# A fused linear-attention and FFN block: another order of transposes, late FFN units and query products

## The chip, the cores and the metric

One core of a Trainium2 chip runs the whole kernel. Its engines work side by side and meet through semaphores: TensorE (matrix products and transposes; PE in the profile, its weight loads PEld), VectorE (DVE), ScalarE (ACT), GpSimd (POOL) and SyncE (SP, which issues the DMA transfers). The metric is the device time of one execution in microseconds. Before the change it is 151.27 us, the median of three runs (151.26 to 151.32).

## What is computed

A token matrix x (2048 tokens, width 448) is layer-normalised, and three things are summed: x itself, a linear attention with 16 heads of width 28, and an FFN of width 1792.

```python
xn = _layernorm(x, axis=-1)
return x + _A_ref(xn, A_wqkv, A_w_phi, A_wo) + _B_ref(xn, B_w1, B_w2)
# A, for each head: pq = q @ w_phi, pk = k @ w_phi
phi_q = concat([softmax(pq), softmax(-pq)]);  phi_k = concat([softmax(pk), softmax(-pk)])
kv  = einsum("bhsf,bhsd->bhfd", phi_k, v);    z = einsum("bhsf->bhf", phi_k)
num = einsum("bhqf,bhfd->bhqd", phi_q, kv);   den = einsum("bhqf,bhf->bhq", phi_q, z) + 1e-6
A   = (num / den) @ wo
# B: silu(xn @ w1) @ w2
```

The key-value sums run over all tokens, so no attention output can be formed until the last keys are in.

## The kernel before

**Tiles.** The 2048 tokens are 16 tiles of 128, taken as 8 pairs. TensorE works with its rows in two halves, upper and lower 64, each with its own weights, so one "step" is two products that run side by side into two neighbouring PSUM banks. A contraction over 448 columns takes seven steps in two passes, 4 and then 3 (`contract`, L476); the second pass waits until the first is through. PSUM has eight banks of 512 fp32 columns, and nearly all waits of TensorE are for a bank that ScalarE or VectorE hasn't emptied yet.

**Stages on TensorE, in order.** First, each pair is normalised on VectorE (`ln_stats`, `ln_norm`, L617 to L634; for pairs 0 and 1 `lnz_norm`, L651), transposed on TensorE (`xnT_tr`) and evicted to the buffer xnT (`ln_ev`, `lnz_ev`), while FFN1 units (`ffn1_single`, `ffn1_chunk`) use the pairs that are ready; each unit is emptied by a SiLU on ScalarE. In the same stretch the weights w_phi are folded into those of queries and keys (`fold_tr`, `fold`). Second, for each pair the key, value and query projections (`k_macro`, `q_group`, `q_half`), exponentials on ScalarE, key softmax on VectorE and GpSimd, and key-value sums in one PSUM bank (`k_acc`). Third, the middle: the last FFN1 units ("late units"), the key-value sums transposed (`kv_transpose`) and evicted to KVZ, and the query products of pairs 0 and 1 (`q_products`). Fourth, for each pair the FFN's second product and the output projection, accumulated in one bank pair and stored (`out_pair`, `out_last`), with the query products two pairs ahead.

**Query products and their division.** `q_products(p)` writes, for tile t of the pair, 8 steps into the banks 2 + 2t and 3 + 2t. `q_divide(p)` then works on VectorE: reciprocal (L1145), Dd, den, rden, Gq (to L1155), and one large product from PSUM into the SBUF buffer o_both (L1160). For pair 0 it does all of this for one tile after the other, for pair 1 the factors for both tiles and then the large product by tile, for later pairs everything for both tiles. The large product empties the banks. GpSimd then sums the two softmax halves (L1182).

**What sets the order.** A small planner (`schedule`, L218) places every operation with rough costs; each engine runs its list in that order and waits for semaphores where a dependency crosses engines. On TensorE the planner has little to choose, as written-out lists (`order0`, L871 to L880; `mid`, L931; `chain`, L1056 to L1066 and L1265) fix the sequence through order-only dependencies. On VectorE and ScalarE it chooses, except where such a dependency (`odeps`) ties two operations. The late units are `u[0]` to `u[7]`; `u[i][0]` holds the first pass of unit i (for `u[3]` and later 4 steps of 512 columns), `u[i][1]` the second pass (3 steps). `uu[0]` to `uu[3]` are the query products of pair 0 tile 0, pair 0 tile 1, pair 1 tile 0, pair 1 tile 1.

**Other lines that matter.** `tr1` (L869) are the eight transposes of pair 1, four for each tile; `tr2` and `tr3` (L878) the seven of pairs 2 and 3. Transposes of one pair need different column pieces of the normalised tiles, which VectorE writes one by one. `ln_later` (L884) adds the later pairs; pairs 4 and 5 use the same banks for their transposes. Transfers `q_move` (L1024) rearrange query rows inside SBUF; `moved` (L1267) hangs their waits on late units. SyncE ends with one wait for each output slot (L1340).

```python
order0 += [a[0], b[0], a[1], b[1][:2], c[0], b[1][2:], tr1[:4], c[1][:-1], d[0], tr1[4:], c[1][-1:], d[1]]   # L871
order0[-2:] = [tr2, c1[:4], tr3, c1[4:], d1]                                                                 # L880
chain += [u[0][0], u[1][0], u[0][1], u[2][0], u[1][1], u[2][1], kv, u[3][0], kv_tr, u[3][1], u[4][0], uu[0], # L1265
          u[4][1], u[5][0], uu[1], u[5][1], u[6][0], uu[2], u[6][1], u[7][0], uu[3], u[7][1]]
```

Of the kernel before, what the change touches and what calls it, by code (L numbers as in the profile page):

```python
# [332 lines left out]
def bass_parallel_sum__linear_kernel_hedgehog__dense_activation_silu__prompt_kernel(  # L333
# [10 lines left out]
    S, D, H, DH, FF = 2048, 448, 16, 28, 1792  # L344
# [11 lines left out]
    with es:  # L356
# [303 lines left out]
        def lnz_bank(p, t, j):  # L660
            return 6 if p else ((4, 0) if t == 0 else (6, 2))[j // 2]

# [66 lines left out]
        def ln_pair(p, one_by_one=False, ev=True):  # L729
            t0, t1 = 2 * p, 2 * p + 1  # L730
            for t in (t0, t1):
                ln_stats(t)
                if one_by_one:
                    ln_rstd(t, t + 1)
            if not one_by_one:
                ln_rstd(t0, t1 + 1)
            ln_norm(p, t0)
            ln_norm(p, t1)
            b0 = {2: 0, 3: 2, 6: 0, 7: 0}.get(p, 6)
            ln_tr(p, [0, 1, 2, 3, 4, 5, 6], b0, 448 if p == 7 else 0)  # L740
            if ev:
                ln_ev(p, 0, 7, b0, "act" if p in LN_ACT else "dve")
# [69 lines left out]
        def fold_tr(w0):  # L812
            for w in range(w0, w0 + 3):
                for kt in range(4):
                    c = ((w - w0) * 4 + kt) * 64
                    c0 = 0 if w == 0 else 112 * w - 64
                    trs([(bank16[6 + h][:, c:c + 64], wraw[r, kt, c0:c0 + 128], r)
                         for h, r in ((0, UP), (1, LO))], "wT_tr")
            for h in range(2):
                src = bank16[6 + h][:, 0:768].rearrange("p (w k u) -> p w k u", w=3, k=4)  # L820
                dst = wT[:, w0:w0 + 3, :].rearrange("p w (k b u) -> p w b k u", b=2, u=64)[:, :, h]
                copy_dve(dst, src, "wT_ev", d_dve(768, 2))

        def fold(kt):
            bA, bB = banks[6], banks[7]
# [21 lines left out]
        banks_ = iter((4, 0, 2, 4, 0, 2, 4, 6))  # L847
        evp, passes, ln_late = [], [], []
# [44 lines left out]
        def last_xn(ops):  # L893
            return [o for o in ops if o.name == "xn"][-1].id
# [10 lines left out]
        ffn1_chunk(2, 2, 0, 4, (2, 4, 0))  # L905
        tr5, later5 = ln_later(5, early_dve)
        ftr = []
        for i in range(3):
            ffn1_chunk(2, 2, 4 + 2 * i, 6 + 2 * i, (2, 4, 0))
            ftr.append(marked(fold_tr, 3 * i))  # L910
        unit_no[0] = 0
        ffn1_chunk(2, 4, 10, FT, (0, 2, 4, 2))
        ffn1_chunk(4, 2, 0, 2, (4,))
        tr6, later6 = ln_later(6, last_xn(later4), False)
# [11 lines left out]
        for kt in range(4):  # L926
            if kt:
                ffn1_chunk(4, 4, 1 + kt, 2 + kt, (0, 2, 4))
            folds.append(marked(fold, kt))
# [18 lines left out]
        def k_macro(p):  # L948
            sl = p % NEK
            kbk = {1: 4, 2: 6, 7: 6}.get(p, 2)  # L950
            k12 = proj(p, lambda r, k: wqk_sb[r, k, 1, :, 0:56], kbk, "pk_mm")
# [24 lines left out]
        def k_acc(p):  # L976

            sl, ops = p % NEK, []
            for t in range(2):
                first, last = p == 0 and t == 0, p == NPAIR - 1 and t == 1  # L980
                E3 = Ek[sl][:, t, :].rearrange("p (s c) -> p s c", s=2)
                for c in range(4):
                    parts = []
                    for i in range(4):
                        h = 4 * c + i
                        parts.append((banks[4][VW * i:VW * i + VW, 56 * c:56 * c + 56].rearrange("p (s f) -> p s f", s=2),
                                      vaug[sl][:, t, h, :], E3[:, :, h * DH:h * DH + DH], first and c == 0, last))
                    ops.append(mms(parts, "kv_mm", 50.0, 32))
            return ops

        def q_group(ch, c):
            qb = {1: 2, 2: 4, 6: 2}.get(4 * ch + c, 6)
            done = contract([(lambda r, b: xnT[r, b, 4 * ch:4 * ch + 4, :].rearrange("p a c -> p (a c)"),
# [7 lines left out]
        def q_half():  # L1001


            qb, done = 6, []
            for q in range(2):
# [71 lines left out]
        def kv_transpose():  # L1077

            kvT = scr[:, 64:64 + 4 * 112]
            bA = banks[4][:, 0:4 * 56].rearrange("p (a f) -> p a f", a=8)[:, :, None, :].broadcast_to([128, 8, 2, DH])  # L1080
            dA = kvT.rearrange("p (a i f) -> p a i f", a=8, i=2)
# [4 lines left out]
            for s in range(2):  # L1086
                for c in range(4):
                    parts = []
                    for j in range(2):
                        r, o = slice(64 * j, 64 * j + 64), 64 + 112 * c + 56 * s - 64 * j  # L1090
                        parts.append((bank16[4 + j][:, (4 * s + c) * 64:(4 * s + c + 1) * 64], scr[r, o:o + 128],
                                      ident[r, 64 * j:64 * j + 64]))
# [8 lines left out]
            for j, eng in ((0, "dve"), (1, "act")):  # L1101
                r = slice(64 * j, 64 * j + 56)
                src = bank16[4 + j][r, 0:512].rearrange("p (a h d) -> p a h d", a=8, h=2)[:, :, :, 0:DV]
# [211 lines left out]
        def emit_engine(ename, eng):  # L1315
# [24 lines left out]
            if ename == "sp":  # L1340
                for i in range(len(out_sems)):
                    if out_cnt[i] > 0:
                        eng.wait_ge(out_sems[i], 16 * out_cnt[i])

# [48 lines left out]
```

## Time and profile before

| what | value |
|---|---|
| median of three runs | 151.27 us |
| the profiled execution | 151.52 us |
| its span, first to last instruction | 149.7 us |
| TensorE busy | 146.1 us |
| VectorE busy | 100.2 us |
| ScalarE busy | 72.5 us |
| GpSimd busy | 56.4 us |
| mean granted TensorE clock | 0.999 |

The profile is one execution, recorded by the hardware. Times in it count from the first instruction. A row of the timeline reads: start, length, engine, source line, operation, output<-inputs, shapes, number of instructions merged into the row, and in brackets the idle time of that engine before it with what ended it. A matrix product's end is modelled, and consecutive products overlap in the pipeline, so TensorE's progress is read from starts: the next group's start less this group's start. A row of the chain reads: start, length, engine, output, line. L448 is the helper that issues all products in halves, L461 the one for transposes, L467 every ScalarE operation, L471 every VectorE copy.

### The profile page before, as it was taken

To read this page: it belongs to the slowest core of one execution; us is meant where nothing else is said; L and a number is where in the kernel's file an instruction comes from. 1 tells how busy PE (TensorE), PEld (TensorE's weight loads), DVE (VectorE), ACT (ScalarE), POOL (GpSimd) and SP (SyncE) were. 2 spreads that over 40 slices of the span, in tenths; PEclk is the share of its full clock that TensorE was granted. 3 is DMA by queue.
4 is the path that set the end of the run, shared out by engine and by line. 5 is a ranking of instruction groups with operands and counts; after the bars stand their busy time and mean duration, and the time that the engine had idled before them with its cause. 6 is when DMAs were issued, how large, how long until landed. Compare 5 with 4: busy or idle time off the path is not lost.

```text
span 149.7 us, 5611 instructions
## 1 busy us (share of the span) xinstructions
PE 146.1 (98%) x2530; PEld 91.6 (61%) x2530; DVE 100.2 (67%) x192; ACT 72.5 (48%) x83; POOL 56.4 (38%) x86
## 2 busy tenths in 40 slices
PE   7999999999999999999999999999999999999992
PEld 6888889557764444444486545555555555555672
DVE  1888898885428899777992677839393939392203
ACT  3647756657799887779488654202020202022000
POOL 7133130210102779876991064270707060614000
PEclk9999999999999999999999999999999999999999
DMA  4999373100004332342201000010101010101012
GB/s 118 352 245 262 90 243 87 49 4 0 4 0 127 123 125 66 89 125 40 44 8 16 4 0 4 0 66 0 66 0 66 0 68 0 66 0 66 0 61 66
DMA packets 9426, 10.29 MB, mean 69 GB/s; under 512 B 1626, under 2 KB 9018, under 8 KB 9402
## 3 DMA queue, kind: packets, MB, share of 16 engines
q1 hardware_dynamic: 9098, 9.71, 22.6%
q8 instruction: 20, 0.33, 0.9%
q10 hardware_dynamic: 304, 0.21, 0.5%
q14 instruction: 4, 0.03, 0.1%
HBM read 7.37 MB, written 1.84 MB: 61 GB/s over the span
## 4 chain that ended last, share of the span: by engine, by line
PE 94%; DVE 3%; issue 0%; DVEq 0%
PE psum L448 91%; PE psum L461 3%; DVE wraw L1160 1%; DVE R L1145 0%; DVE rden L1152 0%; DVE out_raw L1211 0%; DVE Gq L1153 0%; DVE Dd L1147 0%; DVE den L1149 0%; PE psum L1096 0%; DVEq L1333 0%
## 5 line engine op out<-in xcount | busy, mean ns | idle before, releaser
L448 PE MATMUL psum<-w_sb,hT 64*128 64x448 bf16 (+2 forms) x504 | 46.5, 328 | 0.0
L448 PE MATMUL psum<-xnT,w_sb 64*128 64x256 bf16 (+2 forms) x600 | 46.3, 297 | 0.0
L467 ACT ACTIVATE hT<-psum 128x1024 bf16<-128x1024 f32 (+1 forms) x29 | 28.2, 994 | 14.1 <-PE psum L448 11.8
L1182 POOL TENSOR_TENSOR xn_sb<-wraw 128x448 bf16<-128x448 f32 (+4 forms) x39 | 20.7, 562 | 36.3 <-DVE wraw L1160 28.3
L448 PEld LDWEIGHTS psum<-xnT,w_sb 64*128 64x128 bf16 x600 | 27.9, 94 | 8.6
L448 PEld LDWEIGHTS psum<-w_sb,hT 64*128 64x128 bf16 x504 | 22.5, 94 | 16.8
L467 ACT ACTIVATE oT<-psum 128x896 bf16<-128x896 bf16 x8 | 7.3, 917 | 40.2 <-PE psum L461 40.2
L971 POOL TENSOR_TENSOR scr<-scr,Rk 128x1792 bf16<-128x1792 bf16 (+2 forms) x8 | 19.2, 2409 | 11.4 <-DVE Rk L965 7.9
L1160 DVE TENSOR_TENSOR wraw<-psum,Gq 128x1792 f32<-128x1792 f32 (+1 forms) x10 | 16.4, 1650 | 0.8
L467 ACT ACTIVATE EqT<-psum 128x1024 bf16<-128x1024 f32 x14 | 13.6, 1022 | 4.0 <-PE psum L448 4.0
L1211 DVE TENSOR_TENSOR out_raw<-psum,x_sb 128x896 bf16<-128x896 f32 (+2 forms) x9 | 8.8, 980 | 9.5 <-PE psum L448 9.4
L1145 DVE RECIPROCAL R<-psum 128x64 f32<-128x64 f32 (+1 forms) x9 | 4.6, 512 | 15.3 <-PE psum L448 15.3
L448 PE MATMUL psum<-wv_sb,xnT 64*128 64x448 bf16 x112 | 13.9, 349 | 0.0
L448 PE MATMUL psum<-wo_sb,oT 64*128 64x448 bf16 (+2 forms) x126 | 13.6, 328 | 0.0
L448 PE MATMUL psum<-wqk_sb,xnT 64*128 64x448 bf16 x112 | 13.4, 349 | 0.0
L625 POOL TENSOR_TENSOR rstd<-ve,neghalf 128x2 f32<-128x2 f32 (+1 forms) x9 | 6.0, 661 | 19.1 <-DVE ve L624 19.1
L448 PE MATMUL psum<-xnT,wqk_sb 64*128 64x512 bf16 (+1 forms) x112 | 13.0, 378 | 0.0
L963 DVE TENSOR_REDUCE Sk<-scr 128x64 f32<-128x1792 bf16 (+1 forms) x8 | 12.3, 1534 | 0.2
L610 DVE BATCH_NORM_STATS2 st<-x_sb 128x6 f32<-128x448 bf16 x16 | 9.8, 617 | 3.4 <-DMA x_sb<-in_A_x_dram 3.4
L467 ACT ACTIVATE scr<-psum 128x896 bf16<-128x896 f32 x12 | 10.3, 912 | 2.2 <-PE psum L448 1.8
L471 DVE CAST scr<-psum 128x896 bf16<-128x896 f32 x6 | 6.5, 1081 | 5.8 <-PE psum L448 5.8
L448 PEld LDWEIGHTS psum<-wo_sb,oT 64*128 64x128 bf16 x126 | 5.9, 94 | 4.8 <-ACT oT L467 0.2
(78 smaller groups left out, 136.5 us busy)
## 6 DMA issues: line engine op xcount, KB each, us to landing
out_dram<-out_raw SPq DMA_DIRECT2D x7, 224.0 KB, 1.9
w_sb<-in_B_w_dram SPq DMA_DIRECT2D x3, 448.0 KB, 3.3
x_sb<-in_A_x_dram SPq DMA_DIRECT2D x2, 448.0 KB, 4.8
w_sb<-in_B_w_dram SPq DMA_DIRECT2D x2, 384.0 KB, 6.1
x_sb<-in_A_x_dram SPq DMA_DIRECT2D x3, 224.0 KB, 5.5
w_sb<-in_B_w_dram SPq DMA_DIRECT2D x3, 224.0 KB, 4.3
wraw<-in_A_wqkv_dram SPq DMA_DIRECT2D x1, 672.0 KB, 4.5
w_sb<-in_B_w_dram SPq DMA_DIRECT2D x1, 576.0 KB, 4.6
```

The lines of the kernel that those rows point to most:

```text
L448: r = e.matmul(dst, lhsT, rhs, start=start, stop=stop, skip_group_check=True)
L461: out = e.transpose(dst, src, ident[r, 64:128] if r == LO else ident[r, 0:64])
L467: return P.op("act", d_act(_cols(src)), lambda e: e.activation(dst, src, func, scale=scale), reads=[src], writes=[dst], table=table, name= ...
L471: return P.op("dve", dur, lambda e: e.tensor_copy(dst, src), reads=[src], writes=[dst], name=name)
L610: P.op("dve", 600, lambda e: e.bn_stats(st6[:, t, :], x_sb[:, t, :]), reads=[x_sb[:, t, :]], writes=[st6[:, t, :]], name="bnst")
L625: P.op("pool", 580, lambda e: e.tensor_tensor(r2, v2, nh, ALU.pow), reads=[v2, nh], writes=[r2], name="rstd")
L963: P.op("dve", d_dve(896 * n), lambda e, S4=S4, E4=E4: e.tensor_reduce(S4, E4, AXL.X, ALU.add), reads=[E4], writes=[S3], name="Sk")
L971: lambda e, E5=E5, R5=R5: e.tensor_tensor(E5, E5, R5, ALU.mult),
L1145: P.op("dve", d_rec(32 * n), lambda e, R3=R3, U=U: e.reciprocal(R3, U[:, :, :, DH + 1]), reads=[U[:, :, :, DH + 1]], writes=[r2], name="R2")
L1160: P.op("dve", d_dve(896 * m), lambda e, dsto=dsto, Uj=Uj, Gj=Gj, m=m: e.tensor_tensor(dsto, Uj[:, :, :, 0:DH], Gj[:, :, :, None].broadcast ...
L1182: lambda e, dst=dst, a0=a0, a1=a1: e.tensor_tensor(dst, a0, a1, ALU.add),
L1211: P.op("dve", d_dve(2 * (c1 - c0)), lambda e: e.tensor_tensor(dst, ob, xs, ALU.add), reads=[ob, xs], writes=[dst], name="out_ev")
```

## The change

The diff has six parts.

- **Banks.** In everything up to the key-value transposes, banks 4 and 5 change places with banks 6 and 7. The query products stay in banks 2 to 5. The last five FFN1 units take the banks 4, 0, 6, 0, 6, where they took 6, 0, 6, 0, 6.
- **Late units.** After the key-value transposes, TensorE does the first pass of `u[4]` and one step of `u[3]`'s second pass, then `uu[0]`, then the other two steps.
- **Early transposes.** Pair 1's fourth transpose and pair 3's last three move behind one and two steps of FFN1.
- **Pair 4.** Its eviction on VectorE comes behind pair 5's normalisation.
- **Waits for moved query rows.** The last two, of fifteen, now hang on `u[5]`'s second pass.
- **The last waits of SyncE** come in the order in which the output slots are last used.

A helper `u_view` replaces the slice of the view `U4`. The diff, without the lines that only rename banks:

```diff
-            b0 = {2: 0, 3: 2, 6: 0, 7: 0}.get(p, 6)
+            b0 = {2: 0, 3: 2, 6: 0, 7: 0}.get(p, 4)
...
-        order0 += [a[0], b[0], a[1], b[1][:2], c[0], b[1][2:], tr1[:4], c[1][:-1], d[0], tr1[4:], c[1][-1:], d[1]]
+        order0 += [a[0], b[0], a[1], b[1][:2], c[0], b[1][2:], tr1[:3], c[1][:1], tr1[3:4], c[1][1:-1], d[0], tr1[4:], c[1][-1:], d[1]]
...
-        order0[-2:] = [tr2, c1[:4], tr3, c1[4:], d1]
+        order0[-2:] = [tr2, c1[:4], tr3[:4], c1[4:6], tr3[4:], c1[6:], d1]
...
-        evp.append(later4[-1])
+        ev4 = later4[-1]
+        evp.append(ev4)
...
         tr5, later5 = ln_later(5, early_dve)
+        ev4.odeps.add(last_xn(later5))
...
-                        parts.append((banks[4][VW * i:VW * i + VW, 56 * c:56 * c + 56].rearrange("p (s f) -> p s f", s=2),
+                        parts.append((banks[6][VW * i:VW * i + VW, 56 * c:56 * c + 56].rearrange("p (s f) -> p s f", s=2),
...
-        U4 = psum[:, UB * 512:UB * 512 + 2048].rearrange("p (q c) -> p q c", q=4)[:, :, 0:480].rearrange("p q (h c) -> p q h c", c=DZ)
+        def u_view(t, n):
+            return psum[:, (UB + 2 * t) * 512:(UB + 2 * t + 2 * n) * 512].rearrange("p (q c) -> p q c", q=2 * n)[:, :, 0:480].rearrange(
+                "p q (h c) -> p q h c", c=DZ)
...
-                U = U4[:, 2 * t0:2 * t1]
+                U = u_view(t0, n)
...
-        ffn1_chunk(6, 2, 0, 2, (6,))
+        ffn1_chunk(6, 2, 0, 2, (4,))
...
-        ffn1_chunk(4, 4, 5, 10, (6, 0))
+        ffn1_chunk(4, 4, 5, 10, (4, 0, 6, 0, 6))
...
-        chain += [u[0][0], u[1][0], u[0][1], u[2][0], u[1][1], u[2][1], kv, u[3][0], kv_tr, u[3][1], u[4][0], uu[0],
+        chain += [u[0][0], u[1][0], u[0][1], u[2][0], u[1][1], u[2][1], kv, u[3][0], kv_tr, u[4][0], u[3][1][:1], uu[0], u[3][1][1:],
                   u[4][1], u[5][0], uu[1], u[5][1], u[6][0], uu[2], u[6][1], u[7][0], uu[3], u[7][1]]
...
-        for o, d in zip(u[1][0] + u[0][1][:1] + u[5][0], moved):
+        for o, d in zip(u[1][0] + u[0][1][:1] + u[5][0] + u[5][1], moved):
...
-                for i in range(len(out_sems)):
-                    if out_cnt[i] > 0:
-                        eng.wait_ge(out_sems[i], 16 * out_cnt[i])
+                slots = [ops[oid].out_slot for oid in order["sp"] if ops[oid].is_dma]
+                last_use = {i: n for n, i in enumerate(slots) if i is not None}
+                for i in sorted(last_use, key=last_use.get):
+                    eng.wait_ge(out_sems[i], 16 * out_cnt[i])
```

More of the change, by code (lines that the diff above doesn't have):

```diff
@@ L660, in lnz_bank @@
         def lnz_bank(p, t, j):
-            return 6 if p else ((4, 0) if t == 0 else (6, 2))[j // 2]
+            return 4 if p else ((6, 0) if t == 0 else (4, 2))[j // 2]
         def lnz_tr(p, t):
@@ L816, in fold_tr @@
                     c0 = 0 if w == 0 else 112 * w - 64
-                    trs([(bank16[6 + h][:, c:c + 64], wraw[r, kt, c0:c0 + 128], r)
+                    trs([(bank16[4 + h][:, c:c + 64], wraw[r, kt, c0:c0 + 128], r)
                          for h, r in ((0, UP), (1, LO))], "wT_tr")
             for h in range(2):
-                src = bank16[6 + h][:, 0:768].rearrange("p (w k u) -> p w k u", w=3, k=4)
+                src = bank16[4 + h][:, 0:768].rearrange("p (w k u) -> p w k u", w=3, k=4)
                 dst = wT[:, w0:w0 + 3, :].rearrange("p w (k b u) -> p w b k u", b=2, u=64)[:, :, h]
@@ L824, in fold @@
         def fold(kt):
-            bA, bB = banks[6], banks[7]
+            bA, bB = banks[4], banks[5]
             for w in range(9):
@@ L846, in bass_parallel_sum__linear_kernel_hedgehog__dense_activation_silu__prompt_kernel @@
         ev0, order0 = lnz_first()
-        banks_ = iter((4, 0, 2, 4, 0, 2, 4, 6))
+        banks_ = iter((6, 0, 2, 6, 0, 2, 6, 4))
         evp, passes, ln_late = [], [], []
@@ L901, in bass_parallel_sum__linear_kernel_hedgehog__dense_activation_silu__prompt_kernel @@
         tr4, later4 = ln_later(4, early_dve)
-        evp.append(later4[-1])
+        ev4 = later4[-1]
+        evp.append(ev4)
         k = len(units_done)
         unit_no[0] = 0
-        ffn1_chunk(2, 2, 0, 4, (2, 4, 0))
+        ffn1_chunk(2, 2, 0, 4, (2, 6, 0))
         tr5, later5 = ln_later(5, early_dve)
+        ev4.odeps.add(last_xn(later5))
         ftr = []
         for i in range(3):
-            ffn1_chunk(2, 2, 4 + 2 * i, 6 + 2 * i, (2, 4, 0))
+            ffn1_chunk(2, 2, 4 + 2 * i, 6 + 2 * i, (2, 6, 0))
             ftr.append(marked(fold_tr, 3 * i))
         unit_no[0] = 0
-        ffn1_chunk(2, 4, 10, FT, (0, 2, 4, 2))
-        ffn1_chunk(4, 2, 0, 2, (4,))
+        ffn1_chunk(2, 4, 10, FT, (0, 2, 6, 2))
+        ffn1_chunk(4, 2, 0, 2, (6,))
         tr6, later6 = ln_later(6, last_xn(later4), False)
@@ L949, in k_macro @@
             sl = p % NEK
-            kbk = {1: 4, 2: 6, 7: 6}.get(p, 2)
+            kbk = {1: 6, 2: 4, 7: 4}.get(p, 2)
             k12 = proj(p, lambda r, k: wqk_sb[r, k, 1, :, 0:56], kbk, "pk_mm")
@@ L991, in q_group @@
         def q_group(ch, c):
[L992 removed]
+            qb = {1: 2, 2: 6, 6: 2}.get(4 * ch + c, 4)
             done = contract([(lambda r, b: xnT[r, b, 4 * ch:4 * ch + 4, :].rearrange("p a c -> p (a c)"),
@@ L1001, in q_half @@
         def q_half():
-            qb, done = 6, []
+            qb, done = 4, []
             for q in range(2):
@@ L1079, in kv_transpose @@
             kvT = scr[:, 64:64 + 4 * 112]
-            bA = banks[4][:, 0:4 * 56].rearrange("p (a f) -> p a f", a=8)[:, :, None, :].broadcast_to([128, 8, 2, DH])
+            bA = banks[6][:, 0:4 * 56].rearrange("p (a f) -> p a f", a=8)[:, :, None, :].broadcast_to([128, 8, 2, DH])
             dA = kvT.rearrange("p (a i f) -> p a i f", a=8, i=2)
@@ L1090, in kv_transpose @@
                         r, o = slice(64 * j, 64 * j + 64), 64 + 112 * c + 56 * s - 64 * j
-                        parts.append((bank16[4 + j][:, (4 * s + c) * 64:(4 * s + c + 1) * 64], scr[r, o:o + 128],
+                        parts.append((bank16[6 + j][:, (4 * s + c) * 64:(4 * s + c + 1) * 64], scr[r, o:o + 128],
                                       ident[r, 64 * j:64 * j + 64]))
```

4 lines of the change are left out of this document (2 added, 2 removed).

## The prediction

> **What bounds the kernel now.** I read the page's totals first, then the chain that ended last (its shares, then its pieces in order of time), then the timeline around each place where the chain leaves TensorE or where the change touches TensorE's order.
>
> ```profile
> span 149.7 us, 5611 instructions
> ...
> PE 146.1 (98%) x2530; PEld 91.6 (61%) x2530; DVE 100.2 (67%) x192; ACT 72.5 (48%) x83; POOL 56.4 (38%) x86
> ...
> PE 94%; DVE 3%; issue 0%; DVEq 0%
> ...
> 83.50 0.37 DVE R L1145
> ...
> 85.94 0.28 DVE R L1145
> ...
> 88.39 0.05 issue
> ```
>
> TensorE is busy for 98% of the span and carries 94% of the chain. The chain leaves it for one long stretch, VectorE from 83.50 to 88.39: factors and products of pair 0, tile 0 and then tile 1. So only two things shorten the kernel: fewer stretches in which TensorE stands, and a shorter end after its last product. I judge the change by the stops that it removes and the waits that would stand next.
>
> **The late stop (query products).** The timeline of that stretch. "u3", "u4" and so on are the late FFN1 units, each 4 + 3 steps of two 512-column products; uu0 to uu3 are the four blocks of query products (pair 0 tile 0, pair 0 tile 1, pair 1 tile 0, pair 1 tile 1).
>
> ```profile
> 78.46 2.85 ACT L467 ACTIVATE hT<-psum 128x1024 bf16<-128x1024 f32 x3
> 79.68 0.57 PEld L448 LDWEIGHTS psum<-scr 128*32 128x32 bf16 x64 [0.21 <-issue]
> ...
> 81.45 1.68 PE L448 MATMUL psum<-xnT,w_sb 64*128 64x512 bf16 x14
> 81.75 0.56 ACT L467 ACTIVATE KVZ<-psum 56x464 bf16<-56x464 bf16 x1 [0.43 <-PE psum L1096]
> ...
> 82.33 1.02 ACT L467 ACTIVATE hT<-psum 128x1024 bf16<-128x1024 f32 x1
> 82.96 0.39 PE L448 MATMUL psum<-KVZ,EqT 56*128 56x60 bf16 x16
> ...
> 84.71 0.39 PE L448 MATMUL psum<-KVZ,EqT 56*128 56x60 bf16 x16
> 84.94 1.68 PE L448 MATMUL psum<-xnT,w_sb 64*128 64x512 bf16 x14
> 86.46 0.39 PE L448 MATMUL psum<-KVZ,EqT 56*128 56x60 bf16 x16
> 86.69 1.68 PE L448 MATMUL psum<-xnT,w_sb 64*128 64x512 bf16 x14
> 88.43 0.28 PEld L448 LDWEIGHTS psum<-KVZ,EqT 56*128 56x128 bf16 x16 [0.55 <-DVE wraw L1160]
> 88.97 0.56 DVE L1145 RECIPROCAL R<-psum 128x64 f32<-128x64 f32 x1 [0.60 <-PE psum L448]
> ```
>
> Seven steps between two blocks take 84.94 to 86.46, 1.52 us (0.217 a step). The seven from 86.69 are over at 88.21; uu3 begins at 88.43. So TensorE stands 0.22. The row says 0.55, since a load is normally issued a step early. uu3 overwrites tile 1's banks, which VectorE releases at 88.39.
>
> The change swaps the order: after the key-value transposes come u4's first 4 steps, one step of u3's second half, uu0, then u3's last two steps. Before uu0 stand 5 steps in place of 7, so it starts 2 x 0.217 = 0.43 earlier, at 82.53. The VectorE chain hangs on uu0 (83.50, then without a pause to 88.39), so it ends at 87.96; TensorE, ready at 88.21, no longer waits: **-0.22 us**. The rest of the 0.43 isn't gained, since no step is removed and uu1 and uu2 keep their places. For tile 1 VectorE wants uu1 at 85.94 - 0.43 = 85.51. uu1 is over at 84.71 + 0.39 = 85.10, and 0.15 later, as from uu0's end (82.96 + 0.39) to 83.50, VectorE may begin: 85.25. That holds, with 0.26.
>
> Four waits could stand in the stop's place:
> - uu0 needs ScalarE's half of the key-value eviction: 81.75 + 0.56 = 82.31, against 82.53. Spare 0.22.
> - u4 now starts at 81.45 in bank 0, which the third SiLU of the row at 78.46 frees at 81.31. Spare 0.14, the tightest; a signal takes about 0.05 (88.39 to 88.43), which leaves 0.09.
> - Renaming banks (4,5 for 6,7) is a pure exchange up to here, but the query products stay in 2 to 5. So uu1 overwrites bank 4 just after u3 used it, where it overwrote the key-value banks. u3 ends at 82.53 + 0.23 (uu1's length, 84.71 to 84.94) + 2 x 0.217 = 83.19. Before, its last step was over at 81.45 + 3 x 0.217 = 82.10 and its SiLU began at 82.33, 0.23 later; now that SiLU runs from 83.42 to 84.44, against uu1 at 84.71. Spare 0.27.
> - u4's SiLU queues behind it, to 84.44 + 1.02 = 85.46 at worst, and u6 wants bank 0 at 84.94 + 3 x 0.217 = 85.59. Spare 0.13; three in a row take 2.85, 0.95 each, so 85.39 is likelier.
>
> These all hang on TensorE's own times just before, so they move with it. Pair 1's factors (88.97) began 0.60 after VectorE was free: they follow uu3 and come 0.22 earlier too, and everything behind them. GpSimd's sum of pair 0 comes 0.43 earlier, which nothing wants sooner.
>
> **The early stops (transposes of pairs 1 and 3).**
>
> ```profile
> 8.62 0.60 DVE L656 TENSOR_SCALAR EqT<-x_sb,mv,rstd 128x448 bf16<-128x448 bf16 x2
> 9.06 0.41 PE L461 MATMUL psum<-ident,EqT 64*128 64x64 bf16 x8
> ...
> 10.73 0.28 PE L461 MATMUL psum<-ident,EqT 64*128 64x64 bf16 x8
> ...
> 12.75 0.63 DVE L610 BATCH_NORM_STATS2 st<-x_sb 128x6 f32<-128x448 bf16 x1 [0.27 <-DMA x_sb<-in_A_x_dram]
> ...
> 14.94 1.38 DVE L632 TENSOR_SCALAR xn_sb<-x_sb,mv,rstd 128x64 bf16<-128x64 bf16 x5
> 15.45 0.40 PE L461 MATMUL psum<-ident,xn_sb 64*128 64x64 bf16 x14
> ...
> 16.12 0.53 PE L461 MATMUL psum<-ident,xn_sb 64*128 64x64 bf16 x14
> ...
> 16.71 0.62 DVE L471 COPY xnT<-psum 128x896 bf16<-128x896 bf16 x1 [0.39 <-PE psum L461]
> ...
> 17.79 4.97 PE L448 MATMUL psum<-xnT,w_sb 64*128 64x256 bf16 x88
> ...
> 22.59 0.37 PE L461 MATMUL psum<-ident,xn_sb 64*128 64x64 bf16 x14
> ```
>
> Four transposes (x8) take 0.28 undisturbed and 0.41 at 9.06: 0.13 is a stop before the fourth, whose columns end at 8.62 + 0.60 = 9.22. Seven (x14) take 0.37 undisturbed and 0.53 at 16.12: 0.16 is a stop before the fifth, whose columns end at 14.94 + 1.38 = 16.32. The change puts one 256-column step (half of 0.217, 0.11) before pair 1's fourth transpose and two (0.22) before pair 3's fifth; they fill the stops.
>
> Pair 3's is gained. The same VectorE run also holds pair 2's transposes (0.40 at 15.45, 0.03 over 0.37), and TensorE's work from there to the stop is unchanged, so it arrives no sooner than now: **-0.15 us** (0.16 less 0.01 for two more hand-overs). Pair 1's isn't: VectorE stands at 12.75 for a transfer of x and from there runs to 16.32 on its own, so a TensorE that is 0.11 earlier stops 0.11 longer at 15.45. I take **0**; bounds 0 and -0.11.
>
> Pair 3's last transposes end some 0.07 later, so the copy at 16.71 ends at 17.40, not 17.33; its first reader moves from 17.79 to 17.64. Spare 0.24.
>
> **Pair 4's eviction behind pair 5's normalisation.**
>
> ```profile
> 22.04 0.18 DVE L614 BATCH_NORM_AGGREGATE mv<-st 128x2 f32<-128x6 f32 x1
> 22.29 0.40 DVE L632 TENSOR_SCALAR xn_sb<-x_sb,mv,rstd 128x448 bf16<-128x448 bf16 x1
> ...
> 23.10 0.63 DVE L471 COPY xnT<-psum 128x896 bf16<-128x896 bf16 x1 [0.41 <-PE psum L461]
> 23.64 0.58 DVE L632 TENSOR_SCALAR xn_sb<-x_sb,mv,rstd 128x64 bf16<-128x64 bf16 x2
> ...
> 24.13 0.62 DVE L610 BATCH_NORM_STATS2 st<-x_sb 128x6 f32<-128x448 bf16 x1
> ...
> 24.33 0.37 PE L461 MATMUL psum<-ident,xn_sb 64*128 64x64 bf16 x14
> ```
>
> VectorE now idles 0.41 before the copy. After: columns to 22.29 + 0.40 + 0.58 = 23.27, then the copy, to 23.90. Pair 5's transposes use the same bank and wait for it: 23.95 with the signal, against 24.33 - 0.15 = 24.18. Spare 0.23, where the last columns (24.22) would have left almost none. **0** by itself; it keeps the 0.15 from being stopped here. The load of the value weights, paced by this copy, goes out on SyncE's queue 0.17 later (23.90 for 23.73); its first reader, pair 0's value projection, stands behind all FFN1 units of this phase, and the loads queued behind it are needed later still.
>
> **The end, the moved waits, the rest.** SyncE closes with its waits in two instructions and a branch.
>
> ```profile
> L1343 SPq EVENT_SEMAPHORE  x2: 17/22/28, 149.2 to 149.2; - x2
> ...
> L1345 SPq COMPARE_BRANCH  x1: 33/33/33, 149.3 to 149.3; - x1
> ...
> xnT<-xnT SPq DMA_DIRECT2D x1, 32.0 KB, 3.2
> ...
> L1028 SPq DMA_DIRECT2D EqT<-EqT x15: 685/686/1526, 59.8 to 77.9; - x15
> ```
>
> In last-use order the slot that lands last is no longer followed by slots that landed long ago: one instruction fewer after the landing, **-0.05** (bounds 0 and -0.1, the way from 149.2 to 149.3). The last two transfers of query rows are awaited in u5's second half (after 84.94) in place of pair 4's products. The last issue is at 77.9; with the 3.2 of the nearest transfer inside SBUF it lands at 81.1: 0. The query banks' new view names the same addresses, and pair 1's products were by tile before: 0.
>
> **The sum.** -0.22 - 0.15 - 0.05 = -0.42 us. The profiled execution took 151.52 (span 149.7 and 1.8 around it); the median is 151.27, 0.25 less. All terms lie inside the span, so I take them off the median: 150.85, and a span of about 149.3.
>
> **A rule against it.** The change adds four hand-overs between transposes and products (two blocks cut in two). "TensorEngine Tiling (Array Packing)" of the Trainium skill, under Key Properties, has a change of tiling mode drain TensorE. The trace agrees at 79.68, where 64-row work gives way to 128*32 with 0.21 idle. Transposes and products here both read 64*128, so by the rule as worded nothing is added; whoever reads a drain into each hand-over gets the last rival below.
>
> **Rivals.**
> - *The other early gain stays too.* If x lands 0.11 sooner in unprofiled runs, pair 1's stop is gained as well: 150.74. Against it: the wait at 12.75 lasts 0.27.
> - *The late stop only moves.* SiLUs of u3 and u4, now back to back, release bank 0 after u6 wants it, or the one before u4 is late; spares of 0.13 and 0.14 decide. Lost up to 0.22: 151.07.
> - *Only the end is left.* That, and the early 0.15 is stopped again at pair 5's transposes: 151.27 - 0.05 = 151.22.
> - *Slower.* The planner places VectorE's statistics, not the diff. If it puts one tile's (0.62 at 24.13, and 0.18 to aggregate as at 22.04) ahead of pair 4's postponed copy, the copy ends at 23.90 + 0.80 = 24.70, and pair 5's transposes, due at 24.18, stand 0.57 with the signal: 151.27 - 0.42 + 0.57 = 151.42. It decides once the copy is 0.23 late. Against it: the copy is ready at 23.10, before VectorE is.
> - *Every added hand-over drains.* Four at the idle 0.21 of 79.68: +0.84, so 151.69. Against it: the undisturbed rows at 10.73 and 22.59, between products.
>
> **How the numbers follow.** Forecast 0.64 (own range 150.75 to 151.0), other early gain 0.08, late stop moves 0.13, only the end 0.06, slower 0.06, drains 0.03. What this kernel's measurement can tell from no change is about 0.2%, 0.30 us: faster means below 150.97. Faster is 0.64 + 0.08 less 0.01 for the forecast's edge, 0.71; within, 0.13 + 0.06 + 0.01 = 0.20; slower, 0.09. The range takes in the first three cases with the bounds of the unsure terms: 150.68 to 151.12.
>
> **What would show it.** Right: no wait on VectorE's L1160 before the fourth block of query products, and R of pair 0 beginning 0.4 earlier beside an unmoved second block; pair 3's transposes in two groups with no stop; pair 2's transposes stopping 0.1 longer than now. Wrong: a weight load that waits for a SiLU near 81.4, 84.7 or 85.6, pair 5's transposes waiting for a copy at 24.2, or as much time as now from the last landing to SyncE's branch.

## The result and the profile after

The changed kernel takes 150.88 us against 151.27, each the median of 13 runs taken in turn: ratio 0.9976, 95% interval 0.9967 to 0.9985, so -0.36 us with bounds of -0.50 and -0.23 (the two medians are 0.39 apart). Forecast were 150.85 and -0.42; the range of 150.68 to 151.12 holds the time.

The totals of the profile of after:

```profile
span 148.9 us, 5610 instructions
...
PE 145.1 (97%) x2530; PEld 91.0 (61%) x2530; DVE 100.0 (67%) x192; ACT 72.4 (49%) x83; POOL 56.4 (38%) x86
...
PE 94%; DVE 2%; DMA 1%; issue 0%
```

The amounts of work are those of before (the same 2530 products, one instruction fewer in all). The span is 0.75 shorter, more than the medians differ, since the two profiled executions aren't medians: that of before took 151.52, 0.25 above its median, that of after 150.68, 0.20 below. In the chain VectorE falls from 3% to 2%; its pieces are now in the first 5.6 us, and one of 0.42 at 146.30, behind TensorE's last product. The stretch from 83.50 to 88.39 on VectorE has left the chain.

**The late stop is gone.** Timeline of after, the middle (L1160 of before is now L1165, L1145 is L1150):

```profile
80.72 0.29 PEld L1098 LDWEIGHTS psum<-ident,scr 64*128 64x128 bf16 x16 [0.36 <-DVE scr L1084]
81.27 0.56 ACT L467 ACTIVATE KVZ<-psum 56x464 bf16<-56x464 bf16 x1 [0.43 <-PE psum L1098]
81.87 0.45 PEld L448 LDWEIGHTS psum<-KVZ,EqT 56*128 56x128 bf16 x16 [0.16 <-ACT KVZ L467]
82.05 0.39 PE L448 MATMUL psum<-KVZ,EqT 56*128 56x60 bf16 x16
82.58 0.36 DVE L1150 RECIPROCAL R<-psum 128x32 f32<-128x32 f32 x1 [0.91 <-PE psum L448]
84.22 0.39 PE L448 MATMUL psum<-KVZ,EqT 56*128 56x60 bf16 x16
85.97 0.39 PE L448 MATMUL psum<-KVZ,EqT 56*128 56x60 bf16 x16
86.20 1.69 PE L448 MATMUL psum<-xnT,w_sb 64*128 64x512 bf16 x14
86.36 1.09 DVE L1165 TENSOR_TENSOR wraw<-psum,Gq 128x896 f32<-128x896 f32 x1
87.72 0.39 PE L448 MATMUL psum<-KVZ,EqT 56*128 56x60 bf16 x16
87.96 0.82 PE L448 MATMUL psum<-xnT,w_sb 64*128 64x512 bf16 x6
```

From the start of the key-value transposes (here 80.72) to the first query block there are now 82.05 - 80.72 = 1.33 us, where before there were 1.76. The seven steps before the fourth block run from 86.20 to 87.72, exactly their 1.52, and VectorE's large product ends at 87.45, before it is wanted. From the transposes to the unit step behind the fourth block it is 87.96 - 80.72 = 7.24 (7.233 to the nanosecond), against 7.469 before: **-0.236**. Below this is called the late stretch. The bracket at 81.87 isn't a loss: a load is normally issued a step ahead, and here it comes 0.18 ahead instead.

**The early stops.** Timeline of after, pairs 1 to 5:

```profile
8.88 0.26 PE L461 MATMUL psum<-ident,EqT 64*128 64x64 bf16 x6
8.97 0.28 PE L448 MATMUL psum<-xnT,w_sb 64*128 64x256 bf16 x2
9.09 0.20 PE L461 MATMUL psum<-ident,EqT 64*128 64x64 bf16 x2
...
12.20 0.63 DVE L610 BATCH_NORM_STATS2 st<-x_sb 128x6 f32<-128x448 bf16 x1
14.40 1.38 DVE L632 TENSOR_SCALAR xn_sb<-x_sb,mv,rstd 128x64 bf16<-128x64 bf16 x5
15.15 0.37 PE L461 MATMUL psum<-ident,xn_sb 64*128 64x64 bf16 x14
...
15.79 0.28 PE L461 MATMUL psum<-ident,xn_sb 64*128 64x64 bf16 x8
15.91 0.38 PE L448 MATMUL psum<-xnT,w_sb 64*128 64x256 bf16 x4
16.13 0.25 PE L461 MATMUL psum<-ident,xn_sb 64*128 64x64 bf16 x6
...
22.11 0.37 PE L461 MATMUL psum<-ident,xn_sb 64*128 64x64 bf16 x14
...
23.84 0.37 PE L461 MATMUL psum<-ident,xn_sb 64*128 64x64 bf16 x14
```

Every group follows without a gap. Pair 3's stop is filled, and so is pair 1's. Against the forecast, pair 2's transposes (15.15) aren't stopped either: VectorE's statistics, which stood 0.27 for x at 12.75 before, ran at 12.20 with no wait. From pair 1's first transpose to pair 4's first it is 22.11 - 8.88, 13.235 in full, against 13.529 before: -0.29. Below this is called the early stretch.

**The end.** VectorE's last row in the timeline of before, then in that of after:

```profile
146.05 1.38 DVE L1211 TENSOR_TENSOR out_raw<-psum,x_sb 128x640 bf16<-128x640 f32 x2 [4.67 <-PE psum L448]
```

```profile
145.35 1.37 DVE L1216 TENSOR_TENSOR out_raw<-psum,x_sb 128x640 bf16<-128x640 f32 x2 [4.67 <-PE psum L448]
```

From there to the end of the span, which is the closing waits and what follows them, it takes 2.255 before and 2.205 after: **-0.05**.

These three make -0.236 - 0.294 - 0.05 = -0.58 of the 0.75 between the two spans. The remaining 0.17 is 0.19 ahead of 9 us (pair 1's transposes start at 8.88 instead of 9.06), where the change only renames banks, less 0.02 lost in small amounts elsewhere; the section on the hardware returns to it.

### The profile page after: what moved, and what is told of

Same layout as the page of the kernel before. It is cut to its first block, busy times and chain, and to the rows that moved or that the text cites. A ratio compares the mean times of both kernels' runs of the same rounds, so it can differ in the third digit from the quotient of the medians.

```text
span 148.9 us, 5610 instructions
## 1 busy us (share of the span) xinstructions
PE 145.1 (97%) x2530; PEld 91.0 (61%) x2530; DVE 100.0 (67%) x192; ACT 72.4 (49%) x83; POOL 56.4 (38%) x86
## 4 chain that ended last, share of the span: by engine, by line
PE 94%; DVE 2%; DMA 1%; issue 0%
PE psum L448 91%; PE psum L461 3%; DMA x_sb<-in_A_x_dram 1%; DVE st L610 1%; DVE EqT L656 1%; DVE out_raw L1216 0%; DVE mv L614 0%; PE psum L1098 0%; DVE rstd L694 0%
## 5 line engine op out<-in xcount | busy, mean ns | idle before, releaser
L1165 DVE TENSOR_TENSOR wraw<-psum,Gq 128x1792 f32<-128x1792 f32 (+1 forms) x10 | 16.4, 1650 | 0.9
L1150 DVE RECIPROCAL R<-psum 128x64 f32<-128x64 f32 (+1 forms) x9 | 4.6, 512 | 15.0 <-PE psum L448 15.0
L471 DVE CAST scr<-psum 128x896 bf16<-128x896 f32 x6 | 6.5, 1081 | 5.8 <-PE psum L448 5.8
```

Of the source, the lines that this page charges most:

```text
L471: return P.op("dve", dur, lambda e: e.tensor_copy(dst, src), reads=[src], writes=[dst], name=name)
L1150: P.op("dve", d_rec(32 * n), lambda e, R3=R3, U=U: e.reciprocal(R3, U[:, :, :, DH + 1]), reads=[U[:, :, :, DH + 1]], writes=[r2], name="R2")
L1165: P.op("dve", d_dve(896 * m), lambda e, dsto=dsto, Uj=Uj, Gj=Gj, m=m: e.tensor_tensor(dsto, Uj[:, :, :, 0:DH], Gj[:, :, :, None].broadcast ...
```

## The experiments

The theory is the sum's: the late swap removes VectorE's late stop, the early splits remove stops of TensorE that VectorE's columns cause, the reordered closing waits give 0.05, and nothing else matters. The rivals were that the late stop only moves, that renamed banks or added hand-overs change something themselves, and that the early gain isn't there in general. "After" and "before" without more mean the two kernels. Ratios are to the kernel before on the same chip.

**The late part alone.** The changed kernel without the early splits, pair 4's order, the moved waits and the new closing order.

```diff
-        order0 += [..., tr1[:3], c[1][:1], tr1[3:4], c[1][1:-1], d[0], ...]
+        order0 += [..., tr1[:4], c[1][:-1], d[0], ...]
...
-        order0[-2:] = [tr2, c1[:4], tr3[:4], c1[4:6], tr3[4:], c1[6:], d1]
+        order0[-2:] = [tr2, c1[:4], tr3, c1[4:], d1]
...
-        ev4.odeps.add(last_xn(later5))
...
```

> Before plus the late part alone (renamed banks, late units' new order). Theory of the prediction: the stop before the fourth block of query products goes, nothing stands in its place: start of the key-value transposes to the unit step after that block 7.47 us before, 7.25 here; time -0.22, 151.05. Rival (the stop only moves to a SiLU or to the key-value eviction): 7.47 again and 151.27, with a weight load waiting near 81.4, 84.7 or 85.6.

Measured: 151.11 us, ratio 0.9967 (0.9944 to 0.9990); late stretch 7.231. So the late gain comes from the late part alone, and the stop doesn't move to another place. From its timeline:

```profile
8.80 0.66 PEld L448 LDWEIGHTS psum<-xnT,w_sb 64*128 64x128 bf16 x14 [0.76 <-DMA w_sb<-in_B_w_dram]
...
9.69 0.28 PE L461 MATMUL psum<-ident,EqT 64*128 64x64 bf16 x8
...
16.65 0.37 PE L461 MATMUL psum<-ident,xn_sb 64*128 64x64 bf16 x14
...
88.37 0.49 PEld L448 LDWEIGHTS psum<-KVZ,EqT 56*128 56x128 bf16 x16
```

The last row is the fourth query block without a wait. The first three hold a surprise: TensorE stood for a load of the FFN weights, and then the undivided transposes of pairs 1 and 3 took their undisturbed 0.28 and 0.37. Where TensorE comes late, VectorE's columns are ready and there is nothing to fill.

**The early part alone.** The kernel before with both splits and pair 4's order.

```diff
-        order0 += [..., tr1[:4], c[1][:-1], d[0], ...]
+        order0 += [..., tr1[:3], c[1][:1], tr1[3:4], c[1][1:-1], d[0], ...]
...
-        order0[-2:] = [tr2, c1[:4], tr3, c1[4:], d1]
+        order0[-2:] = [tr2, c1[:4], tr3[:4], c1[4:6], tr3[4:], c1[6:], d1]
...
+        ev4.odeps.add(last_xn(later5))
```

> Before plus the two split transposes and pair 4's order. Theory of the prediction: pair 3's stop goes (start of pair 2's transposes to the first FFN1 unit of pairs 2 and 3 2.34 us before, 2.19 here) and pair 1's gain is stopped again at pair 2's transposes, whenever VectorE waits for x before it: -0.15, 151.12. Rival (x lands in time, pair 1's gain stays): -0.26, 151.01, and no stop in pair 2's transposes.

Measured: 151.41 us, ratio 0.9991 (0.9971 to 1.0010), late stretch 7.470. The timing can't tell this part from nothing. In the profiled execution, too, a load came late:

```profile
6.44 1.55 PEld L448 LDWEIGHTS psum<-xnT,w_sb 64*128 64x128 bf16 x42 [0.47 <-DMA w_sb<-in_B_w_dram]
...
10.38 0.12 PEld L448 LDWEIGHTS psum<-xnT,EqT 64*128 64x128 bf16 x2 [0.24 <-issue]
```

Its early stretch is 13.405, with 0.15 of it a stop at 10.4.

**Pair 1 not split.** The changed kernel with pair 1's four transposes together.

```diff
-        order0 += [..., tr1[:3], c[1][:1], tr1[3:4], c[1][1:-1], d[0], ...]
+        order0 += [..., tr1[:4], c[1][:-1], d[0], ...]
```

> After with pair 1's four transposes together again. Theory of the prediction: pair 1's stop of 0.11 is back and pair 2's transposes stop 0.11 less: no change from after, 150.88. Rival (x lands in time): 0.11 slower than after, 150.99, and the same transposes of pair 2.

Measured: 151.04 us, ratio 0.9966 (0.9943 to 0.9989). Again TensorE had waited for FFN weights, 0.45 at 8.6, and the undivided transposes of pair 1 showed no stop. This run can't decide what the split is worth.

**Without pair 4's order.**

```diff
-        ev4.odeps.add(last_xn(later5))
```

> After without the order between pair 4's eviction and pair 5's normalisation. Theory of the prediction: pair 5's transposes come 0.15 earlier and then stop up to 0.1 for their last columns: 150.88 to 150.98. Rival: the copy waits for pair 4's transposes, which come earlier as well, so the columns move with them and nothing stops: 150.88.

Measured: 151.28 us, ratio 0.9982 (0.9961 to 1.0003). From its timeline:

```profile
23.64 0.88 DVE L632 TENSOR_SCALAR xn_sb<-x_sb,mv,rstd 128x448 bf16<-128x448 bf16 x3
24.32 0.52 PE L461 MATMUL psum<-ident,xn_sb 64*128 64x64 bf16 x14
24.68 1.04 PE L448 MATMUL psum<-xnT,w_sb 64*128 64x256 bf16 x16
```

Pair 5's columns end at 23.64 + 0.88 = 24.52, after its transposes began, and these take 0.36 to the next step where the kernel after takes 0.20 to 0.21 (23.84 to 24.05). A stop of 0.14 in the place where the prediction saw "almost none" left. So this line of the change gains nothing by itself and keeps what pair 3's split gains.

**Only the banks.** The changed kernel with the old order of the late units.

```diff
-        chain += [..., kv_tr, u[4][0], u[3][1][:1], uu[0], u[3][1][1:],
+        chain += [..., kv_tr, u[3][1], u[4][0], uu[0],
```

> After with the late units in the order of before, so of the late part only the renamed banks are left. Theory of the prediction: renaming costs and gains nothing, the stop before the fourth block of query products is back: start of the key-value transposes to the unit step after that block 7.47 (after 7.23). Rival (the banks carry part of the gain): between 7.23 and 7.47.

Measured: late stretch 7.466, one run of 151.37 us. The old stop is back:

```profile
88.42 0.29 PEld L448 LDWEIGHTS psum<-KVZ,EqT 56*128 56x128 bf16 x16 [0.54 <-DVE wraw L1165]
```

The renaming is neutral; the order makes the gain.

**The first query block two steps earlier still.**

```diff
-        chain += [..., kv_tr, u[4][0], u[3][1][:1], uu[0], u[3][1][1:],
+        chain += [..., kv_tr, u[4][0][:3], uu[0], u[4][0][3:], u[3][1],
```

> After with the first block of query products behind 3 unit steps in place of 5. By the prediction's row for ScalarE's half of the key-value eviction (0.22 spare) TensorE is there 0.43 sooner and waits 0.2 to 0.26 for it, with nothing more to gain later: the stretch from the key-value transposes to the step after the fourth block 7.44 to 7.49 (after 7.23). Rival (the eviction is seen sooner than the row's end says): 7.23.

Measured: late stretch 7.502, one run of 151.22 us.

```profile
82.15 0.28 PEld L448 LDWEIGHTS psum<-KVZ,EqT 56*128 56x128 bf16 x16 [0.59 <-ACT KVZ L467]
```

Now ScalarE's half of the key-value eviction is late by 0.26, with two steps (0.43) less ahead of the block than the kernel after has, so 0.17 of them were spare. The spare of 0.22 was 0.05 too high, which is why the stretch came out just above the expected 7.44 to 7.49. The change sits at the edge of what the eviction allows.

**Fewer, larger key-value blocks.** An attempt to gain more. Each block of key-value products (shape 128*32) is preceded by some 0.09 more than a step takes. The kernel after, with six changes of shape fewer by joining blocks of neighbouring pairs.

```diff
-                chain += [k12[0], v12[0], k12[1], v12[1], k_acc(3)]
+                chain += [k12[0], v12[0], k12[1], v12[1]]
...
-                chain += [k12[0], k_acc(4), v12[0], k12[1], v12[1], q12[0], k_acc(5), q12[1]]
+                chain += [k12[0], k_acc(3) + k_acc(4), v12[0], k12[1], v12[1][:1], q12[0], v12[1][1:], q12[1]]
+            elif p == 5:
+                chain += [k12[0], v12[0], k12[1], v12[1], q12[0], k_acc(1) + k_acc(2), q12[1]]
...
-        kv = k_acc(NPAIR - 2) + k_acc(NPAIR - 1)
+        kv = k_acc(NPAIR - 3) + k_acc(NPAIR - 2) + k_acc(NPAIR - 1)
```

> After with the key-value products in four blocks (pair 0; 1 and 2; 3 and 4; 5, 6 and 7) in place of seven. In the trace of before and of after TensorE stands 0.09 us at each change between 64-row work and these 128*32 products; three blocks fewer are six changes fewer. Theory (each change has that price, whatever stands around it): 6 x 0.094 = 0.56 less than after, 150.3, if no value projection then waits for the bank that VectorE empties. Rival (the gap is the wait for something else, or the bank wait takes its place): 150.88, with TensorE waiting for VectorE's copy L471 at pairs 5 and 7.

Measured: 151.08 us, ratio 0.9986 (0.9966 to 1.0006): no gain over the kernel after. The stretch from the first fold to the key-value transposes grew, from 46.95 to 47.08. TensorE's waits for VectorE's copy L471 didn't (three, 0.6 in all, in both kernels), so the rival of the bank isn't it. In the timeline of after a single block, and the block of 64 with which both before and after end the key-value sums; then a joined one:

```profile
65.45 0.39 PE L448 MATMUL psum<-scr 128*32 128x56 bf16 x32
65.78 0.82 PE L448 MATMUL psum<-xnT,wqk_sb 64*128 64x512 bf16 x6
...
79.20 0.68 PE L448 MATMUL psum<-scr 128*32 128x56 bf16 x64
79.82 1.04 PE L448 MATMUL psum<-xnT,w_sb 64*128 64x512 bf16 x8
```

```profile
65.35 0.91 PE L448 MATMUL psum<-scr 128*32 128x56 bf16 x64
66.19 0.82 PE L448 MATMUL psum<-xnT,wqk_sb 64*128 64x512 bf16 x6
```

One block of 32 takes 0.33 to the next step, the joined one of 64 takes 0.84, 0.19 more than two. Within it the first 32 weight loads start four every 26 ns, the later ones four every 59 ns, and that costs more than the saved changes of shape. Length alone doesn't make it: the block of 64 at 79.20 takes 0.61, less than two single ones, and its later loads start mostly four every 33 ns. What slows the joined blocks is not shown.

The Trainium skill, "TensorE: Matmul & The Clock Gate", gives TensorE's queue a depth of 64 in the table at its head. 32 loads and 32 products are 64 instructions, which is where the joined block slows down; but the block at 79.20 has as many and doesn't slow down like it, so no run here shows the queue to be the cause.

**TensorE held back, first try.** The kernel before with five more warming products between the transposes of pair 0's tiles.

```diff
-            order = [warm(20), lnz_tr(0, 0), warm(2), lnz_tr(0, 1)]
+            order = [warm(20), lnz_tr(0, 0), warm(7), lnz_tr(0, 1)]
```

> Before with five more warming products (no part of the result) ahead of pair 0's second four transposes, so TensorE is held about 0.5 us at 5.5 us. Theory after the first runs (the stops of pairs 1 and 3 are there only while TensorE is ahead of VectorE; late weights take them away): no stop of 0.11 before pair 1's fourth transpose nor of 0.15 before pair 3's fifth, though neither is split; the span grows by less than the hold. Rival (the stops belong to the order of the transposes): both stops as in before, and the span grows by the whole hold.

Measured: one run of 151.45 us; pair 1's stop still 0.10, pair 3's gone; early stretch 13.324. Mixed: VectorE, which evicts pair 0's second tile, fell back together with TensorE at pair 1 (its columns end at 9.45 for 9.22), and the condition was hardly tested there.

**TensorE held back further, without and with the splits.** Both kernels with eight warming products behind pair 0's transposes. These overwrite bank 2 before VectorE copies the transposes out of it, so that part of pair 0's normalised input is replaced; the instructions are otherwise the same.

```diff
-            order = [warm(20), lnz_tr(0, 0), warm(2), lnz_tr(0, 1)]
+            order = [warm(20), lnz_tr(0, 0), warm(2), lnz_tr(0, 1), warm(8)]
```

> The kernel before with eight more warming products (about 0.107 us each) behind pair 0's transposes, so that TensorE starts FFN1 0.8 us or more later while VectorE and the loads stay where they were. Theory (the early gain is only a stop of TensorE for VectorE's columns, so it is there only while TensorE is ahead): the unsplit transposes of pairs 1 and 3 show no stop (0.28 for x8, 0.37 for x14), and the way from pair 1's first transpose to pair 4's first takes 13.2 to 13.3, as in the split kernel. Rival (VectorE, whose evictions wait for TensorE's transposes, falls back with it): the stops of 0.13 and 0.16 are there as before, 13.5.

> The same eight warming products in the changed kernel. Theory: the way from pair 1's first transpose to pair 4's first is within 0.06 of that of before_late_start (13.2 to 13.3), and the spans of the two differ by the late stop and the end alone, about 0.29. Rival: the splits are worth 0.2 to 0.3 here as well, and the spans differ by 0.5 or more.

Measured: single runs of 152.00 and 151.65 us; early stretch 13.209 without the splits and 13.209 with them. The timeline of the first, which has no split:

```profile
9.98 0.28 PE L461 MATMUL psum<-ident,EqT 64*128 64x64 bf16 x8
...
16.88 0.37 PE L461 MATMUL psum<-ident,xn_sb 64*128 64x64 bf16 x14
```

TensorE came 0.92 later to pair 1 (9.98 for 9.06), VectorE 0.69, and both stops are gone without any split. That settles the early part: the splits shorten nothing themselves, they fill a stop that is there only where TensorE is ahead of VectorE's columns. The other half of the expectation didn't come as stated. The spans differ by 0.35, near the 0.29 of the late stop and the end, but for other reasons: pair 1 begins 0.25 earlier in the second, the end gives 0.06, and the late stretches differ by 0.05 alone (7.371 and 7.325). Without the change VectorE's second large product followed 0.10 sooner on its factor in this program, which shrinks the stop to 0.12, and with the change TensorE stood 0.09 behind the second query block. The traces show the same in both, the order of an instruction's waits. Where it waits for several semaphores, some are awaited by an instruction of their own ahead of it, of 0.05 us. In the kernel before, VectorE's runs at 87.19, behind the factor, and the large product starts 0.13 after the factor's end. In this program it runs while the factor is still being worked out, and the product follows by 0.03 (so too in the first try with five products, whose late stretch is 7.373). With the change it is the step behind the second query block, which waits for a moved query row besides: here the waiting instruction comes at 85.26, at the block's end, where in the kernel after it runs at 84.06, while the block's loads still go out. Why the extra products turn the order of the waits is not shown.

**Both kernels once more.** Unchanged.

> The kernel before, a second look. If the loads of w are in time: 13.53 from pair 1's first transpose to pair 4's first, stops of about 0.1 and 0.16 in the transposes of pairs 1 and 3, and 7.47 from the key-value transposes to the step after the fourth query block. If TensorE waits for a load of w before 9 us, by more than 0.2: no such stops, and about 13.3.

> The changed kernel, a second look: 7.23 for the late stretch and 2.20 from VectorE's last instruction to the end of the span in any case; 13.2 to 13.25 for the early stretch if the loads of w are in time, 13.3 to 13.4 if TensorE waits for one.

Measured: late stretch 7.465 and 7.232, end 2.255 and 2.204, early stretch 13.430 and 13.233, single runs of 151.48 and 151.01 us. Timeline of the kernel before, second profile (lines are one higher here):

```profile
8.32 0.66 PEld L449 LDWEIGHTS psum<-xnT,w_sb 64*128 64x128 bf16 x14 [0.22 <-DMA w_sb<-in_B_w_dram]
9.21 0.28 PE L462 MATMUL psum<-ident,EqT 64*128 64x64 bf16 x8
10.15 0.12 PEld L449 LDWEIGHTS psum<-xnT,EqT 64*128 64x128 bf16 x2 [0.28 <-DMA EqT<-in_B_w_dram]
16.32 0.37 PE L462 MATMUL psum<-ident,xn_sb 64*128 64x64 bf16 x14
```

A late load at 8.3, and both undivided groups run undisturbed, as expected; but then TensorE stands 0.20 for the next load, at 10.18, and the stretch isn't the 13.3 that was expected. The early stretch in all profiles:

| kernel | splits | TensorE's stops inside it | early stretch |
|---|---|---|---|
| before | no | 0.11 pair 1, 0.15 pair 3 (VectorE) | 13.529 |
| before, second profile | no | 0.20 at 10.2 (load) | 13.430 |
| before, held back | no | 0.10 pair 1 (VectorE) | 13.324 |
| before, late start | no | none | 13.209 |
| late part alone | no | none above 0.06 | 13.277 |
| after | yes | none | 13.235 |
| after, second profile | yes | none | 13.233 |
| after, late start | yes | none | 13.209 |
| without pair 4's order | yes | none | 13.210 |
| pair 1 not split | pair 3 | 0.09 at 10.4 (the same as below) | 13.321 |
| only the banks | yes | 0.09 at 10.1 (the same as below) | 13.352 |
| first query block two steps earlier | yes | 0.08 at 9.9 (the same as below) | 13.335 |
| early part alone | yes | 0.15 at 10.4 (issue, ahead of a load's first reader) | 13.405 |
| joined key-value blocks | yes | 0.25 at 11.6 (the same) | 13.467 |

No split kernel stands for VectorE's columns inside this stretch. Against the one profile of before that stood for no load the splits give 0.29; with late loads they give less, since the load takes the time first. Two split kernels, the banks alone and the earlier query block, stood 0.15 for VectorE ahead of pair 1's *first* transpose instead: the next place where VectorE can be late.

VectorE's own progress is the other half of the condition. In the first profile of before it had stood 0.27 for x at 12.75, and pair 3's last columns ended at 16.32; in the second one and with five more warming products it had no such wait, and they ended at 16.19 and 16.20, 0.25 and 0.24 before TensorE came to them. So that stop needs TensorE early and VectorE late, and no run here holds one of the two fixed. All these stops are for columns or for loads; of the stops of before that are followed here only the late one is for a bank.

## Why the prediction was right, point by point

- **The late stop, -0.22.** Right, as argued: 0.236 in the profile, 0.238 with the late part alone, and 0.233 between the second profiles. The four steps behind it held: the first block came 0.43 earlier against the transposes (1.33 for 1.76), the second block kept its place, the eviction's spare of 0.22 was real, if nearer to 0.17 (0.26 of stop with 0.43 less), and none of the waits for ScalarE at u4, the second block or u6 appeared. The rival that the stop only moves is refuted.
- **Pair 3's stop, -0.15.** Right for the execution that was profiled (both profiles of the kernel after run without a stop, where the first of the kernel before stands 0.15), but the step that took it as there in every execution failed: in four of the five profiles with an undivided pair 3 the stop was absent. There a late load (two) or my added warming products (two) had put TensorE later, and VectorE had not stood for x at 12.75.
- **Pair 1's stop, 0.** This step was wrong for the same kind of reason. It rested on VectorE's wait for x at 12.75, from which pair 2's transposes would have been stopped instead. In both profiles of the kernel after VectorE has no such wait and pair 2's transposes are undisturbed, so the 0.11 stays gained where the stop exists. The rival with the other early gain had this mechanism; its 150.74 was not the median.
- **The early sum.** The late part and the end are 0.29 of the measured 0.36; what is left for the early parts is 0.07, with bounds of -0.06 and 0.21 from the ratio's interval. The predicted 0.15 lies within, the 0.29 of the first pair of profiles doesn't. The runs of the parts can't divide the time more finely: the late part alone gave 0.9967, the early part alone 0.9991, with intervals more than 0.003 wide. So a gain of the early part in the median is not shown. Two errors of opposite sign, a gain too few and a condition overlooked, made the sum come out near, and that is luck.
- **Pair 4's order, 0 by itself.** Right, and what it guards is 0.14. The rival that statistics slip ahead of the postponed copy didn't happen: pair 5's transposes run at 23.84 without a wait.
- **The end, -0.05.** Right: 2.255 to 2.205, and the same 0.05 in the second profiles. The five profiles with the old closing order have 2.255 to 2.269, the nine with the new one 2.201 to 2.206.
- **Banks, moved waits, hand-overs, 0.** The banks are neutral by the run with the old order. The added hand-overs between transposes and products cost nothing that the timeline shows (15.91, 16.13 and 8.97 follow at their usual distances), so the rival of 151.69 is refuted. Its 0.21 was the idle time of a load; from product to product the change of shape at 79.68 costs 0.09 (0.20 for 0.11). The moved waits weren't tried alone; no row of the unaltered kernel after waits for them, but in its late-start program one cost the 0.09 above.

## What to carry to other kernels

Price a stop together with the condition that makes it: TensorE stood for VectorE only where nothing had delayed TensorE before, and the one stop at pair 3 came where VectorE had also waited for x. A gain read from one profile at a place behind the first loads is a gain in part of the executions, and two or three profiles show it. A stop deep in the kernel, whose both sides hang on the same start, gave the same 0.23 to 0.24 between all profiles of the two kernels and of their parts. When work is moved to fill a stop, ask what arrives earlier behind it: here one eviction's order had to be changed, or the 0.14 would have been stopped again at the next pair.

## What the runs showed of the hardware that was not expected

- **The first loads don't land alike.** TensorE's wait for FFN weights between 6 and 9 us ranged from nothing to 0.65 from profile to profile, and a wait for the next load at 10 to 12 us came in some. How much of the spread of single runs (150.65 to 151.31 for the kernel after) that makes is not shown: both profiles of the kernel after were without such a wait, and took 150.68 and 151.01.
- **The warming products differ as well.** The timeline's row of them in the first profile of the kernel after, then in that of before:

```profile
3.14 1.59 PE L448 MATMUL psum<-const-bfloat16-1.0 64*128 64x256 bf16 x18
```

```profile
3.14 2.15 PE L448 MATMUL psum<-const-bfloat16-1.0 64*128 64x256 bf16 x18
```

The same 18 products, nine steps, take 1.59 and 2.15. Their starts in the traces show why. In both, the steps begin 0.213 us apart at first, half the pace of later steps of this width (0.11). In after the pace doubles at 4.0 us, in before only at about 6.0, behind the warming products. The granted clock prints 1.00 over both stretches, but its record begins only at 4.01 and 6.07, so it says nothing about what lies ahead. The other profiles with such a record have the change between 3.6 and 6.6 us. In before, the chain that ended last starts with these products (0.84 to 5.29), in after with the first load of x and with VectorE. In the second profile of after, where the pace changes at 5.97, pair 1 begins at 9.10, as late as in before. So the late change of pace fits the 0.19 by which pair 1 begins later in before; it wasn't tried by itself, and what sets its time is not shown.
- **The waits of one instruction have an order.** Where the separate waiting instruction comes behind the work that could have hidden it, it cost 0.10 us on VectorE and 0.09 on TensorE.
- **Some runs of small products slow down** after their first 32 loads, to four every 59 ns in place of 26, and others of the same length don't; the cause stays open.
